# K and Q stored with the head's dimension first: PE's transposes of them against DMAs between halves of SBUF

## The chip, the cores and the metric

The kernel runs on one core of a Trainium2 chip. The metric is the device time of one execution in microseconds (us). All matrix work is done by TensorE (PE, with its weight loads shown as PEld); VectorE (DVE), ScalarE (ACT) and GpSimd (POOL) do the rest, and SyncE (SP) issues every DMA.

## The reference

Attention with pooled queries, then two feed-forward layers. B, H, S, D = 2, 8, 1152, 64.

```python
q_pool = q.reshape(B, H, S // 2, 2, D).mean(axis=3)
scores = scale * np.matmul(q_pool, k.transpose(0, 1, 3, 2))
attn = softmax(scores)                      # over S = 1152 keys
x = np.matmul(attn, v)                      # (B, H, 576, D) -> (1152 tokens, 512)
h = x @ w_in;  g = h * tanh(softplus(h));  x = g @ w_out      # 512 -> 2048 -> 512
h = x @ w_in2; g = elu(h);                 out = g @ w_out2
```

All tensors are float32 outside; the weights come as 64-bit floats and are converted on the chip.

## The kernel before

The attention goes through 8 pairs of heads (`n`). A pair has 9 query tiles of 128 rows: four of head 0 and four of head 1, alternating, and a last one made of the two heads' 64 remaining queries (`order`). The loop `while s < len(tiles)` takes one such tile as a step `s`, and each step works on several tiles at once: `qk` multiplies tile s (three blocks of 384 keys, in `A` banks of PSUM), DVE's `scores` scales it into `sp` and takes the maximum, ACT's `exp(s - 1)` and POOL's `norm(s - 1)` finish the tile before, and `trans(s - 3)` turns the tile three steps back on PE (in `B` banks), from which `probs` copies it to `pt`. `av` multiplies the turned probabilities with V; it runs in steps 1, 3, 5 and 8 of a pair, in portions of 8 or 10 products. Programs are in order on each engine; there is no planner here, and the order of the calls in the loop is the order on each engine.

The products of Q and K are made exact enough by splitting every number in two float32r halves, high and low. K is the moving operand: `KA` holds head 0's high half in partitions 0 to 63 and its low half in 64 to 127, `KB` head 1's, the other way round. Q is the stationary operand: `Q[h, 0]` is the high half of head h in both halves of the partitions, `Q[h, 1]` the low half.

K and Q come from memory with the tokens in the partitions. So for the next pair, in steps 3, 7 and 8 (`prep_k`) and 5 and 10 (`prep_q`), PE turns 9 blocks of K and 4.5 of Q into the single `D` bank; ACT rounds the high halves out of it (L246, L272), DVE subtracts for the low halves (L248, L274), and POOL copies each Q half to the other half of the partitions (L281). `pool_q` adds neighbouring queries first, on POOL (L229). In the steps with such work DVE, not ACT, copies the middle third of `probs` (`more`).

Eight chunks of weights are also converted during the attention (`Weights`: read in step 7 of a pair, `rebias` on ACT two steps later, `clamp` on POOL, `shift` and `words` on DVE, `high` on ACT, `rest` on POOL). `mlps` does the two layers in 48 units each; a unit is 12 products of `h_mm` (L172) and 9 or 12 of `out_mm` (L573), with the chunks converted ahead through a ring of NR = 4 raw buffers.

Of the kernel before, what the change touches and what calls it, by code (L numbers as in the profile page):

```python
# [22 lines left out]
def tile_pool_attention_mish_elu_mlp(  # L23
# [13 lines left out]

    nc = tc.nc
    B, H, S, D = q.shape
    NT, DM = out.shape  # L40
    DFF = moe_w_in.shape[1]
    P = 128
# [15 lines left out]
    NR = 4  # L58
# [83 lines left out]
    BANKS = {"A": 3, "B": 3, "C": 1, "D": 1}  # L142
    sums = cycle(("B", "B", "B", "C", "D"))
# [33 lines left out]
    def attention():  # L177
        with ExitStack() as st:
            ap = st.enter_context(tc.tile_pool(name="attn", bufs=2))
            pools["f"] = st.enter_context(tc.tile_pool(name="f1", bufs=2))  # L180
            raw_k, raw_q, ks, qs_t, vs = {}, {}, {}, {}, {}

            def load_k(n, pieces=1):
                b, h0 = n // NP, 2 * (n % NP)
                raw_k[n] = ap.tile([P, KT, 2, D], F32, tag="kr", name="kr", bufs=1)
                w = KT // pieces
                for c in range(pieces):
                    for h in range(2):
                        src = k[b, h0 + h].rearrange("(p t) d -> p t d", p=P)
                        t = slice(c * w, (c + 1) * w)  # L190
                        yield nc.sync.dma_start(out=raw_k[n][:, t, h, :], in_=src[:, t, :])

            def load_q(n, pieces=1):
                b, h0 = n // NP, 2 * (n % NP)
                qr = ap.tile([P, 2, 2 * NQ, D], F32, tag="qr", name="qr", bufs=1)
                qe = ap.tile([QR, 2, 2, D], F32, tag="qe", name="qe", bufs=1)
                raw_q[n] = [qr, qe]
                src = q[b, h0:h0 + 2, :2 * NQ * P].rearrange("h (p r) d -> p h r d", p=P)
                w = 2 * NQ // pieces
                for c in range(pieces):  # L200
                    r = slice(c * w, (c + 1) * w)
                    yield nc.sync.dma_start(out=qr[:, :, r, :], in_=src[:, :, r, :])
                yield nc.sync.dma_start(
                    out=qe, in_=q[b, h0:h0 + 2, 2 * NQ * P:].rearrange("h (p r) d -> p h r d", r=2)
                )
# [5 lines left out]

            def pool_q(n, eng, heads, t0=0, t1=NQ):

                if n not in qs_t:
                    qs_t[n] = Q = {}
                    raw_q[n] += [
                        ap.tile([P, NQ, 2, D], F32, tag="qs", name="qs", bufs=1),
                        ap.tile([QR, 2, D], F32, tag="qse", name="qse", bufs=1),
                    ]
                    for h in range(2):  # L220
                        for part in range(2):
                            Q[h, part] = ap.tile([P, NQ * P + P], F32R, tag=f"Q{h}{part}", name=f"Q{h}{part}")
                            z0 = NQ * P + (QR if h == 0 else 0)
                            nc.gpsimd.memset(Q[h, part][:, z0:z0 + QR].bitcast(F32), 0.0)
                qr, qe, qs, qse = raw_q[n]
                qv = qr.rearrange("p h (t r) d -> p h t r d", r=2)
                t = slice(t0, t1)
                for h in heads:
                    eng.tensor_tensor(qs[:, t, h, :], qv[:, h, t, 0, :], qv[:, h, t, 1, :], op=ALU.add)  # L229
                if t1 == NQ and 1 in heads:  # L230
                    eng.tensor_tensor(qse, qe[:, :, 0, :], qe[:, :, 1, :], op=ALU.add)


            left = {"act": [], "dve": [], "pool": []}

            def prep_k(n, g, bank="D"):
                kr = raw_k[n]
                if g == 0:
                    ks[n] = [ap.tile([P, S], F32R, tag=t, name=t) for t in ("KA", "KB")]
                KA, KBt = ks[n]  # L240
                pt = psum(bank)
                for i in range(3):
                    nc.tensor.transpose(pt[:, i * P:(i + 1) * P], kr[:, 3 * g + i], ident)  # L243
                c = slice(g * KB, (g + 1) * KB)
                for a, (r, o) in ((KA, (slice(0, D), slice(D, P))), (KBt, (slice(D, P), slice(0, D)))):
                    left["act"].append(lambda a=a, r=r: nc.scalar.copy(a[r, c], pt[r, :KB]))  # L246
                    left["dve"].append(
                        lambda a=a, r=r, o=o: nc.vector.tensor_tensor(a[o, c], pt[r, :KB], a[r, c], op=ALU.subtract)  # L248
                    )

            def prep_q(n, g, bank="D"):
                qs, qse = raw_q[n][2:]
                Q = qs_t[n]
                pt = psum(bank)
                t0, t1 = (0, NQ // 2) if g == 0 else (NQ // 2, NQ)
                w = 0
                for t in range(t0, t1):
                    nc.tensor.transpose(pt[:, w:w + P], qs[:, t], ident)  # L258
                    w += P
                if g == 1:  # L260
                    nc.tensor.transpose(pt[:, w:w + QR], qse, ident[:QR, :QR])  # L261
                    w += QR
                for h in range(2):
                    r, r2 = slice(h * D, (h + 1) * D), slice((1 - h) * D, (2 - h) * D)
                    pieces = [(slice(t0 * P, t1 * P), slice(0, (t1 - t0) * P))]
                    if g == 1:
                        if h == 0:
                            pieces = [(slice(t0 * P, t1 * P + QR), slice(0, w))]
                        else:
                            pieces.append((slice(t1 * P + QR, t1 * P + P), slice(w - QR, w)))  # L270
                    for o, i in pieces:
                        left["act"].append(lambda h=h, o=o, i=i, r=r: nc.scalar.copy(Q[h, 0][r, o], pt[r, i]))  # L272
                        left["dve"].append(
                            lambda h=h, o=o, i=i, r=r: nc.vector.tensor_tensor(  # L274
                                Q[h, 1][r, o], pt[r, i], Q[h, 0][r, o], op=ALU.subtract
                            )
                        )
                    o = slice(pieces[0][0].start, pieces[-1][0].stop)
                    for x in range(2):
                        left["pool"].append(  # L280
                            lambda h=h, x=x, o=o, r=r, r2=r2: nc.gpsimd.tensor_scalar(  # L281
                                Q[h, x][r2, o], Q[h, x][r, o].bitcast(F32), 1.0, 1.0, op0=ALU.mult, op1=ALU.mult
                            )
                        )

            def leave(*engines, most=99):
                for e in engines:
                    for f in left[e][:most]:
                        f()
                    del left[e][:most]  # L290
# [8 lines left out]
            def qk(s, j):  # L299
                n, i = tiles[s]  # L300
                KA, KBt = ks[n]
                Q = qs_t[n]
                sc[s, j] = pt = psum("A")
                c = slice(j * KB, (j + 1) * KB)
                if order[i] is None:
                    cols = slice(NQ * P, NQ * P + P)
                    terms = [(Q[0, 0], KA), (Q[0, 1], KA), (Q[1, 0], KBt), (Q[1, 1], KBt)]
                else:
                    h, t = order[i]
                    cols = slice(t * P, (t + 1) * P)  # L310
                    terms = [(Q[h, 0], (KA, KBt)[h]), (Q[h, 1], (KA, KBt)[h])]
                for x, (qq, kk) in enumerate(terms):
                    nc.tensor.matmul(pt[:, :KB], qq[:, cols], kk[:, c], start=(x == 0), stop=(x == len(terms) - 1))  # L313
# [72 lines left out]
            loads, preps, avs = {}, {}, {}  # L386
            for n in range(n_pairs):
# [6 lines left out]
                if n + 1 < n_pairs:  # L394
                    for r, f in (0, load_k), (-4, load_q):
                        loads.setdefault(s0 + r, []).append(lambda f=f, n=n: list(f(n + 1)))
                    loads.setdefault(s0 + 4 + LAG, []).append(lambda n=n: load_v(n + 1))
                    for r, f, g in zip(
                        (3, 5, 7, 8, 10),
                        (prep_k, prep_q, prep_k, prep_k, prep_q), (0, 0, 1, 2, 1),  # L400
                    ):
                        preps[s0 + r] = (f, n + 1, g)
            going = []
            pieces = [(x, y) for x in range(NW) for y in range(2)]


            kk, qq = load_k(0, 3), load_q(0, 2)
            for g in (qq, kk, kk, kk, kk, kk, kk, qq, qq):
                next(g)
            load_v(0)  # L410
# [297 lines left out]
```

## Time and profile before

| | us |
|---|---|
| median of 3 runs (lowest to highest) | 677.01 (677.01 to 677.14) |
| the profiled execution's own time | 677.06 |
| its span, from the first to the last instruction | 675.3 |
| PE busy | 659.9 (98%) |
| DVE, ACT, POOL busy | 502.6 (74%), 432.0 (64%), 218.7 (32%) |
| granted TensorE clock over the span | 1.00 |

The span is what the engines' records cover; the 1.76 us by which the execution is longer lie before and after them. A share of busy time is an average over the attention, which ends at 270 us, and the two layers. PE's matmuls are pipelined, so what an instruction costs is read from the chain of waits (the distance from one to the next), not from its own duration.

### The profile page before, as it was taken

The page shows a single profiled execution, that of the slowest core. Times are in us where ns is not written, and L with a number is a line of the kernel's source. Part 1 is how long each engine was busy: PE and PEld are TensorE (multiplying, and loading weights), DVE is VectorE, ACT ScalarE, POOL GpSimd, SP SyncE. Part 2 cuts the span into 40 slices and gives each one's busy share as a digit, 9 for nine tenths or more (in the row PEclk, how much of TensorE's full clock was granted, in tenths as well). Part 3 has the DMA queues.
Part 4 walks back from the last instruction along what each step waited for, and adds up shares of the span by engine and source line. Part 5 has one row for each costly group of instructions (what it writes and reads, how often), then busy time and mean ns, then how long its engine had stood idle before and what let it go on. Part 6 is the DMA issues. An engine that isn't in the chain of part 4 may idle for free.

```text
span 675.3 us, 11241 instructions
## 1 busy us (share of the span) xinstructions
PE 659.9 (98%) x3976; PEld 583.0 (86%) x3976; DVE 502.6 (74%) x1273; ACT 432.0 (64%) x895; POOL 218.7 (32%) x294
## 2 busy tenths in 40 slices
PE   6899999999999999999999999999999999999997
PEld 4777777777787776999999999999999999999995
DVE  5988888898989883846645765776987788996553
ACT  5888887888888886643443545445666566665442
POOL 2746566565747454211110431333310011110000
PEclk9999999999999999999999999999999999999999
DMA  6313140504130410413124222222211221200111
GB/s 175 102 37 104 34 123 16 137 15 125 36 102 1 160 33 33 124 64 125 64 62 125 63 94 82 75 94 63 93 64 64 93 94 64 94 33 1 47 48 47
DMA packets 47400, 50.79 MB, mean 75 GB/s; under 512 B 20336, under 2 KB 38256, under 8 KB 47344
## 3 DMA queue, kind: packets, MB, share of 16 engines
q1 hardware_dynamic: 47344, 50.08, 24.1%
q8 instruction: 31, 0.51, 0.3%
q14 instruction: 25, 0.20, 0.1%
HBM read 47.71 MB, written 2.36 MB: 74 GB/s over the span
## 4 chain that ended last, share of the span: by engine, by line
PE 96%; DVE 2%; issue 1%; POOL 0%; DMA 0%; ACT 0%; POOLq 0%
PE A L172 30%; PE B L573 18%; PE A L313 13%; PE C L367 11%; PE B L342 11%; PE D L573 6%; PE C L573 6%; PE D L243 1%; DVE sp L319 1%; PE D L258 1%; DMA qr<-in_q_dram 0%; DVE Q L274 0%; DVE part L598 0%; POOL Q L281 0%; PE D L261 0%
## 5 line engine op out<-in xcount | busy, mean ns | idle before, releaser
L172 PE MATMUL A<-XH,wl 128*128 128x384 f32 x384 | 128.9, 336 | 0.0
L172 PE MATMUL A<-XH,wh 128*128 128x384 f32 x384 | 128.8, 336 | 0.0
L172 PE MATMUL A<-XL,wh 128*128 128x384 f32 x384 | 128.6, 335 | 0.0
L319 DVE TENSOR_SCALAR_CACHE_REDUCE sp<-A 128x384 f32<-128x384 f32 x216 | 113.7, 554 | 17.1 <-PE A L313 13.7
L116 POOL TENSOR_SCALAR wf<-wf 128x512 f32<-128x512 f32 x64 | 42.7, 668 | 253.4 <-ACT wf L112 219.7
L336 POOL TENSOR_SCALAR sp<-sp,stat 128x1152 f32<-128x1152 f32 x72 | 91.8, 1275 | 100.0 <-DVE stat L335 87.8
L342 PE MATMUL B<-ident,sp 128*128 128x128 f32 x648 | 105.7, 273 | 4.3 <-POOL Q L281 3.6
L358 ACT COPY pt<-B 128x384 f32<-128x384 f32 x187 | 81.1, 485 | 23.4 <-PE B L342 22.3
L330 ACT ACTIVATE sp<-sp,stat 128x1152 f32<-128x1152 f32 x72 | 90.9, 1262 | 6.3 <-DVE stat L326 5.7
L342 PEld LDWEIGHTS B<-ident,sp 128*128 128x128 f32 x648 | 80.8, 140 | 14.5 <-POOL Q L281 5.9
L367 PE MATMUL C<-pt,vr 128*64 128x320 f32 (+1 forms) x576 | 76.7, 411 | 0.0
L527 ACT ACTIVATE gh<-A 128x384 fp32r<-128x384 f32 x48 | 23.7, 493 | 80.2 <-PE A L172 80.1
L172 PEld LDWEIGHTS A<-XH,wh 128*128 128x128 f32 x384 | 72.1, 188 | 2.5 <-issue 0.5
L313 PE MATMUL A<-KA,Q 128*128 128x384 f32 x240 | 73.5, 390 | 0.3 <-DVE KA L248 0.2
L172 PEld LDWEIGHTS A<-XL,wh 128*128 128x128 f32 x384 | 72.1, 188 | 1.9
L172 PEld LDWEIGHTS A<-XH,wl 128*128 128x128 f32 x384 | 72.0, 188 | 0.0
L313 PE MATMUL A<-KB,Q 128*128 128x384 f32 x240 | 70.5, 376 | 1.3 <-DVE sp L319 1.3
L367 PEld LDWEIGHTS C<-pt,vr 128*64 128x64 f32 x576 | 38.5, 136 | 27.7 <-issue 5.0
L530 DVE TENSOR_TENSOR gl<-g,gh 128x384 fp32r<-128x384 f32 x48 | 31.1, 649 | 34.7 <-ACT g L528 34.6
L553 ACT CAST gh<-g 128x384 fp32r<-128x384 f32 x48 | 24.7, 514 | 48.1 <-DVE g L547 47.8
L127 DVE SCALAR_TENSOR_TENSOR wf<-raw,wf 128x512 int32<-128x512 int32 x64 | 51.6, 806 | 2.2
L313 PEld LDWEIGHTS A<-KA,Q 128*128 128x128 f32 x240 | 37.6, 196 | 13.8 <-issue 9.5
(109 smaller groups left out, 1317.7 us busy)
## 6 DMA issues: line engine op xcount, KB each, us to landing
raw<-in_moe_w_in_dram SPq DMA_DIRECT2D x32, 512.0 KB, 3.8
raw<-in_moe_w_out_dram SPq DMA_DIRECT2D x32, 512.0 KB, 3.3
vr<-in_v_dram SPq DMA_DIRECT2D x8, 576.0 KB, 4.1
kr<-in_k_dram SPq DMA_DIRECT2D x14, 288.0 KB, 4.0
qr<-in_q_dram SPq DMA_DIRECT2D x7, 512.0 KB, 3.9
out_dram<-part SPq DMA_DIRECT2D x8, 256.0 KB, 2.2
kr<-in_k_dram SPq DMA_DIRECT2D x6, 96.0 KB, 2.8
qr<-in_q_dram SPq DMA_DIRECT2D x2, 256.0 KB, 3.1
```

Source lines behind the costliest of these rows:

```text
L116: nc.gpsimd.tensor_scalar(self.f, self.f, HUGE, -HUGE, op0=ALU.min, op1=ALU.max)
L127: nc.vector.scalar_tensor_tensor(f, self.low, 29, f, op0=ALU.logical_shift_right, op1=ALU.bitwise_or)
L172: nc.tensor.matmul(pt[:, :TB], w[:, kk * P:(kk + 1) * P], x[:, kk, tk], start=(i == 0), stop=(i == len(terms) - 1))
L313: nc.tensor.matmul(pt[:, :KB], qq[:, cols], kk[:, c], start=(x == 0), stop=(x == len(terms) - 1))
L319: nc.vector.tensor_scalar(sp[s][:, j * KB:(j + 1) * KB], sc.pop((s, j))[:, :KB], SCALE, None, op0=ALU.mult, op1=ALU.max, accum_out=stat[s] ...
L330: nc.scalar.activation(sp[s], sp[s], AF.Exp, bias=m[:, 3:4], scale=1.0, accum_out=m[:, 4:5])
L336: nc.gpsimd.tensor_scalar(sp[s], sp[s], m[:, 6:7], 1.0, op0=ALU.mult, op1=ALU.mult)
L342: nc.tensor.transpose(pt[:, x * P:(x + 1) * P], sp[s][:, c:c + P], ident)
L358: copy(dst, src)
L367: nc.tensor.matmul(acc[n, g][h * D:(h + 1) * D, :w], vs[n][:, h, kt, :], pts[n, g][:, kt, h, :], start=(kt == 0), stop=(kt == KT - 1),)
L530: nc.vector.tensor_tensor(gl, g, gh, op=ALU.subtract)
L573: nc.tensor.matmul(pt, l, r, start=(first and i == 0), stop=(final and i == 2))
```

## The change

The host hands K and Q over with the head's dimension first, and Q's even and odd queries apart; the odd heads' Q is rotated by 64 so that its leftover queries come first. PE turns neither. For a next pair, K (both heads, one per half of the partitions) and Q come with one DMA each. POOL adds the query halves, ACT rounds all 128 partitions at once, POOL subtracts, and then SP issues six DMAs from SBUF to SBUF, each of 64 partitions by 4,608 bytes (295 KB): three bring Q's halves of each head into both halves of the partitions, three exchange head 0's low half of K and head 1's high half through the raw buffer. `PREP` gives the step of each. The first pair is loaded instead with every head twice, once into each half, in fourteen DMAs, and needs no moves; the second head's raw tiles borrow `sp` buffers. Besides: the `D` bank goes to `B` (4 banks), the raw ring shrinks from 4 to 3, `probs`' middle third goes to DVE except for three of nine tiles, and the output's rows lie one after another.

```diff
-    NR = 4
+    NR = 3
...
-    BANKS = {"A": 3, "B": 3, "C": 1, "D": 1}
-    sums = cycle(("B", "B", "B", "C", "D"))
+    BANKS = {"A": 3, "B": 4, "C": 1}
+    sums = cycle(("B", "B", "B", "B", "C"))
...
-            pools["f"] = st.enter_context(tc.tile_pool(name="f1", bufs=2))
+            pools["f"] = st.enter_context(tc.tile_pool(name="f1", bufs=1))
...
+            def load_k0(h, blocks=(0, 3)):
+                if h not in raw_k:
+                    raw_k[h] = ap.tile([P, S], F32, tag="sp" if h else "kr", name="kr", bufs=LAG + 1 if h else 1)
+                c = slice(blocks[0] * KB, blocks[1] * KB)
+                for r in range(2):
+                    nc.sync.dma_start(out=raw_k[h][r * D:(r + 1) * D, c], in_=k[0, h, :, c])
...
+            def prep_q0(h, pool, low, cols):
+                x, c, o = raw_q[h], slice(*cols), slice(cols[0] + h * QR, cols[1] + h * QR)
+                hi, lo = (qs_t[0][h][:, part, o] for part in range(2))
+                pool.tensor_tensor(x[:, 0, c], x[:, 0, c], x[:, 1, c], op=ALU.add)
+                nc.scalar.copy(hi, x[:, 0, c])
+                low.tensor_tensor(lo, x[:, 0, c], hi, op=ALU.subtract)
+
+            def prep_k0(h, j):
+                K, c, r = ks[0][h], slice(j * KB, (j + 1) * KB), slice(D, P)
+                nc.scalar.copy(K[:, c], raw_k[h][:, c])
+                nc.vector.tensor_tensor(K[r, c], raw_k[h][r, c], K[r, c], op=ALU.subtract)
...
+            def pool_q(n):
+
+                tiles_of(n)
+                x = raw_q[n]
+                nc.gpsimd.tensor_tensor(x[:, 0], x[:, 0], x[:, 1], op=ALU.add)
+
+            def high_q(n):
+                nc.scalar.copy(qs_t[n][0][:, 0, :SQ], raw_q[n][:, 0])
+
+            def low_q(n, eng):
+                x = qs_t[n][0]
+                eng.tensor_tensor(x[:, 1, :SQ], raw_q[n][:, 0], x[:, 0, :SQ], op=ALU.subtract)
+
+            def move_q(n, i):
+                x, y = qs_t[n]
+                src = x[(0 if i == 2 else D):(D if i == 2 else P), :, :SQ]
+                dst = (y[D:, :, QR:], y[:D, :, QR:], x[D:, :, :SQ])[i]
+                nc.sync.dma_start(out=dst.bitcast(F32), in_=src.bitcast(F32))
+
+            def high_k(n, i):
+                c = slice(i * S // 2, (i + 1) * S // 2)
+                nc.scalar.copy(ks[n][0][:, c], raw_k[n][:, c])
+
+            def low_k(n, i, eng):
+                c = slice(i * S // 2, (i + 1) * S // 2)
+                eng.tensor_tensor(ks[n][1][:, c], raw_k[n][:, c], ks[n][0][:, c], op=ALU.subtract)
+
+            def move_k(n, i):
+
+                (x, y), t = ks[n], raw_k[n][:D]
+                src, dst = ((x[D:], t), (y[:D], x[D:]), (t, y[:D]))[i]
+                nc.sync.dma_start(out=dst.bitcast(F32), in_=src.bitcast(F32))
...
+            PREP = [
+                (0, "pool", pool_q, ()), (1, "act", high_q, ()), (2, "pool", low_q, (nc.gpsimd,)),
+                (3, "sp", move_q, (0,)), (3, "sp", move_q, (1,)), (4, "sp", move_q, (2,)),
+                (2, "act", high_k, (0,)), (3, "act", high_k, (1,)),
+                (3, "pool", low_k, (0, nc.gpsimd)), (4, "pool", low_k, (1, nc.gpsimd)),
+                (5, "sp", move_k, (0,)), (6, "sp", move_k, (1,)), (7, "sp", move_k, (2,)),
+            ]
...
-                    for r, f in (0, load_k), (-4, load_q):
-                        loads.setdefault(s0 + r, []).append(lambda f=f, n=n: list(f(n + 1)))
-                    loads.setdefault(s0 + 4 + LAG, []).append(lambda n=n: load_v(n + 1))
...
+                    for r, f in (-3, load_q), (-1, load_k), (4 + LAG, load_v):
+                        loads.setdefault(s0 + r, []).append(lambda f=f, n=n: f(n + 1))
+                    m = n + 1
+                    for r, e, f, args in PREP:
+                        preps.setdefault((s0 + r, e), []).append(lambda f=f, args=args, m=m: f(m, *args))
...
+            load_q0(0, cut[0])
+            load_k0(0, (0, 1))
+            load_k0(0, (1, 3))
+            load_q0(1, cut[1])
+            load_k0(1)
+            load_q0(0, (cut[0][1], SQ))
+            load_q0(1, (cut[1][1], SQ))
             load_v(0)
...
+            for h in range(2):
+                prep_q0(h, nc.vector if h == 0 else nc.gpsimd, nc.vector, cut[h])
+                for j in range(3):
+                    prep_k0(h, j)
+            for h in range(2):
+                prep_q0(h, nc.gpsimd, nc.gpsimd, (cut[h][1], SQ))
...
-                    if s in preps and 1 == j:
-                        f, n, g = preps.pop(s)
-                        f(n, g)
...
-                    for j in range(3):
-                        if j != 1 or not more:
-                            probs(o, j, nc.scalar.copy)
+                    probs(o, 0, nc.scalar.copy)
+                    probs(o, 2, nc.scalar.copy)
+                for f in by["act"]:
+                    f()
...
-                if old and (1 in [j for _, j in tp]):
-                    probs(o, 1, nc.vector.tensor_copy)
+                if old:
+                    probs(o, 1, nc.scalar.copy if o % NI in (0, 1, 3) else nc.vector.tensor_copy)
+                for e in "dve", "pool", "sp":
+                    for f in by[e]:
+                        f()
```

## Rows read from the trace of the kernel before

**Rows 1.** The page: the chain that ended last, by line.

```profile
PE A L172 30%; PE B L573 18%; PE A L313 13%; PE C L367 11%; PE B L342 11%; PE D L573 6%; PE C L573 6%; PE D L243 1%; DVE sp L319 1%; PE D L258 1%; DMA qr<-in_q_dram 0%; DVE Q L274 0%; DVE part L598 0%; POOL Q L281 0%; PE D L261 0%
```

**Rows 2.** Windows by pair: start:end, length, engines' busy us, clock, DMA share.

```profile
0.00:35.27 35.27, 26.53 (x141) 21.01 (x143) 26.48 (x97) 24.77 (x49) 18.04 (x39) 1.00 0.47 133
...
195.24:227.23 31.99, 31.66 (x230) 24.83 (x231) 28.11 (x103) 27.33 (x58) 19.39 (x26) 1.00 0.32 92
227.23:257.35 30.12, 30.12 (x218) 23.68 (x220) 24.40 (x95) 24.83 (x53) 15.07 (x15) 1.00 0.10 32
```

**Rows 3.** Chain of waits in pair 3: start us, length us, engine, tile, line.

```profile
104.82 0.22 PE D L258 x2
105.04 0.20 PE D L261
105.24 0.48 PE B L342 x3
...
111.56 0.33 PE D L243 x3
...
128.01 0.33 issue
128.34 0.52 PE B L342 x3
```

**Rows 4.** Chain of waits in pair 7, which prepares no next pair's K.

```profile
229.54 0.55 PE A L313 x2
...
231.78 0.35 PE A L313 x2
...
243.39 0.55 PE A L313 x2
```

**Rows 5.** Groups of instructions by line: busy us, mean ns of one, idle before.

```profile
L342 PE MATMUL B<-ident,sp 128*128 128x128 f32 x648 | 105.7, 273 | 4.3 <-POOL Q L281 3.6 <-issue 0.7
...
L135 ACT CAST wh<-wf 128x512 fp32r<-128x512 f32 x64 | 39.7, 620 | 5.2 <-DVE wf L127 5.2
...
L281 POOL TENSOR_SCALAR Q<-Q 64x256 fp32r<-64x256 f32 (+2 forms) x64 | 27.3, 441 | 6.5 <-ACT Q L272 3.9
...
L358 DVE COPY pt<-B 128x384 f32<-128x384 f32 x29 | 16.2, 557 | 0.5
...
L229 POOL TENSOR_TENSOR qs<-qr 128x256 f32<-128x256 f32 (+1 forms) x16 | 13.7, 861 | 1.4 <-DMA qr<-in_q_dram 0.8
...
L138 POOL TENSOR_TENSOR wl<-wf,wh 128x512 fp32r<-128x512 f32 x8 | 10.3, 1281 | 4.6 <-ACT wh L135 4.6
```

**Rows 6.** DMA queue and issues: KB each, median us from issue to landing.

```profile
q1 hardware_dynamic: 47344, 50.08, 24.1%
...
vr<-in_v_dram SPq DMA_DIRECT2D x8, 576.0 KB, 4.1
...
out_dram<-part SPq DMA_DIRECT2D x8, 256.0 KB, 2.2
...
out_dram<-part SPq DMA_DIRECT2D x2, 128.0 KB, 2.3
```

**Rows 7.** Chain of waits of the first 36 us: by line, two steps.

```profile
by line: PE A L313 20.5%; PE B L342 11.3%; DVE sp L319 10.4%; DMA qr<-in_q_dram 7.9%; issue 6.8%; DVE Q L274 6.1%; POOL Q L281 4.9%; DVE KB L248 4.3%; POOL sp L336 3.4%; DVE KA L248 3.2%; PE C L367 2.2%; ACT Q L272 2.1%; PE B L258 1.9%; PE 
...
10.69 0.58 DVE sp L319 x2
...
17.99 0.33 PE B L342 x3
```

**Rows 8.** Timeline of the start: first uses of the two halves of Q.

```profile
3.60 0.49 DVE L229 TENSOR_TENSOR qs<-qr 128x128 f32<-128x128 f32 x2 [3.60 <-DMA qr<-in_q_dram]
...
7.90 0.87 POOL L229 TENSOR_TENSOR qs<-qr 128x128 f32<-128x128 f32 x2 [0.79 <-DMA qr<-in_q_dram]
```

**Rows 9.** Timeline of SP in the second layer: a chunk is read.

```profile
585.78 0.37 SPq L100 DMA_DIRECT2D raw<-in_moe_w_in_dram  x1
```

**Rows 10.** Timeline of ACT there: the chunk before that one is converted.

```profile
591.03 0.68 ACT L112 ACTIVATE wf<-raw 128x512 f32<-128x512 f32 x1 [0.45 <-DVE wl L138]
```

More of the change, by code (lines that the diff above doesn't have):

```diff
@@ L193, in load_q, with tiles_of @@
-            def load_q(n, pieces=1):
-                b, h0 = n // NP, 2 * (n % NP)
[L195 to L205, printed above, removed]
+            def tiles_of(n):
+                ks[n] = [ap.tile([P, S], F32R, tag=t, name=t) for t in ("KA", "KB")]
+                qs_t[n] = [ap.tile([P, 2, SQ + QR], F32R, tag=f"Q{h}", name=f"Q{h}") for h in range(2)]
+                for h in range(2):
+                    z0 = 0 if h else SQ
+                    nc.gpsimd.memset(qs_t[n][h][:, :, z0:z0 + QR].bitcast(F32), 0.0)
@@ new lines, in load_k0, with load_q0 @@
+            def load_k0(h, blocks=(0, 3)):
[4 more added lines that the diff above has]
+                    nc.sync.dma_start(out=raw_k[h][r * D:(r + 1) * D, c], in_=k[0, h, :, c])
+            def load_q0(h, cols):
+                if h not in raw_q:
+                    x = ap.tile([P, S], F32, tag="sp" if h else "qr", name="qr", bufs=LAG + 1 if h else 1)
+                    raw_q[h] = x.rearrange("p (a s) -> p a s", a=2)
+                c = slice(*cols)
+                for r in range(2):
+                    nc.sync.dma_start(out=raw_q[h][r * D:(r + 1) * D, :, c], in_=q[0, h, :, :, c])
@@ new lines, in load_k, with load_q @@
+            def load_k(n):
+                b, h0 = n // NP, 2 * (n % NP)
+                raw_k[n] = ap.tile([P, S], F32, tag="kr", name="kr", bufs=1)
+                nc.sync.dma_start(out=raw_k[n], in_=k[b, h0:h0 + 2].rearrange("h d s -> (h d) s"))
+            def load_q(n):
+                b, h0 = n // NP, 2 * (n % NP)
+                x = ap.tile([P, S], F32, tag="qr", name="qr", bufs=1)
+                raw_q[n] = x.rearrange("p (a s) -> p a s", a=2)
+                nc.sync.dma_start(out=raw_q[n], in_=q[b, h0:h0 + 2].rearrange("h d a s -> (h d) a s"))
@@ L210, in load_v @@
                 nc.sync.dma_start(out=vs[n], in_=v[b, h0:h0 + 2].rearrange("h (p t) d -> p h t d", p=P))
[L212 to L231, printed above, removed]
@@ L234, in attention @@
[L234 to L249, printed above, removed]
@@ L251, in prep_q @@
[L251 to L290, printed above, removed]
             order = [(h, t) for t in range(NQ) for h in range(2)] + [None]
@@ L440, in attention @@
                     av(*a)
-                more = left["dve"] and not any(w.age == 4 for w in going)
+                by = {e: preps.pop((s, e), []) for e in ("act", "dve", "pool", "sp")}
                 if mid:
                     exp(s - 1)
-                leave("act")
                 if old:
-                    for j in range(3):
-                        if j != 1 or not more:
-                            probs(o, j, nc.scalar.copy)
+                    probs(o, 0, nc.scalar.copy)
+                    probs(o, 2, nc.scalar.copy)
+                for f in by["act"]:
+                    f()
                 if new:
@@ L451, in attention @@
                     scores(s, 1)
-                if new:
                     scores(s, 2)
@@ L463, in attention @@
                         tokens(n, g)
-                if 2 <= s % NI < 2+2 and s // NI + 1 < n_pairs:
-                    pool_q(s // NI + 1, nc.gpsimd, (s % NI - 2,))
                 for w in list(going):
```

57 lines of the change are left out of this document (18 added, 39 removed).

## The prediction

> **What bounds the kernel now.** I first read the page's chain that ended last [rows 1]: nearly all of it is PE, and the lines of the attention (L313, L342, L367) are a third. So work taken from PE is worth its time, if nothing else becomes late. To see whether that holds where the change acts, I cut the attention where the av of step 8 begins, once per pair, and read the busy time of each piece [rows 2]. A pair takes 31.99 us and PE is busy for 31.66 of them; DVE is busy for 28.11, ACT for 27.33, POOL for 19.39. Pair 7, the last, has no next pair's K to prepare and only the second half of its own Q: it takes 30.12 us and PE is never idle. That pair is a run of the new PE program which the trace already holds. The chain inside a pair [rows 3, 4] then shows what the 1.87 us between the two consist of.
>
> This document reckons with the profiled execution's own 677.06 us (span 675.3 and 1.76 around it); the median of the runs is 677.01, so the two agree within 0.05.
>
> **What leaves PE.** Three K blocks are one piece of 0.33 us in the chain, three times a pair: 0.98. The second half of Q takes 0.22 and 0.20, and the three probability turns behind it take 0.48 instead of 0.33: 0.57. The first half of Q is two turns like the 0.22. In step 8 PE then waits 0.33 for probabilities, and the turns behind the wait take 0.52 instead of 0.33: 0.52 in all [rows 3]. Of all waits of these turns most is put down to POOL's Q copies, 3.6 us, since POOL's normalisation is queued behind them; the copies go too (L281, 0.44 us each, 8 a pair [rows 5]). Sum: 0.98 + 0.57 + 0.22 + 0.52 = 2.29 us a pair. The windows say the same from the other side: pair 7 without its 0.57 us is 30.12 - 0.57 = 29.55 us, and 31.99 - 29.55 = 2.44. I take 2.44, which holds the small waits as well. Pairs 1 to 6 gain it in full: 6 x 2.44 = 14.6 us. Pair 7 gains 0.57. Sum 15.2 us. The turns of pair 0 are in the start's term below.
>
> **What comes to the other engines.** ACT gets three roundings of 128 x 576 per pair in place of the K and Q roundings; a 128 x 512 one takes 0.62 [rows 5], so 0.7 each, 2.1 in all. Even on top of pair 7's 24.83 us [rows 2] that is 26.9 of 29.55. DVE loses every subtraction for K and Q and gets the middle `probs` copies of six tiles instead of one in pair 7: 24.40 + 5 x 0.56 [rows 2, 5] = 27.2 of 29.55, its Q subtractions not yet taken off. POOL gets one sum and three subtractions of 576 columns. A 128 x 512 two-input instruction takes 1.28 and 256 columns take about 0.86 [rows 5]: 1.4 to 1.9, say 1.5 each, 6 a pair. Against that go its Q copies (8 x 0.44) and sums (2 x 0.9): POOL stays near 20. In the fullest steps (3 and 4) POOL does a normalisation of 1.2, a subtraction of 1.5 and once a weight's 1.28, up to 4.0 us, but a tile's normalisation is called two steps before its turn. So each of them is cheap because PE's work covers it; without the cover ACT would cost most, since it stands ahead of exp.
>
> **The moves.** Each subtraction of low halves ends on POOL, then SP moves 295 KB three times in a row for K, each waiting for the one before. In pair 7 step 0 opens at 229.54, step 1 at 231.78 and step 4 at 243.39 [rows 4]. So step 4 opens 13.85 after step 0; POOL then has its normalisation (1.2) and the last K subtraction (1.5), with some waiting: done at about 17.2. Head 1's K is needed when the next pair's step 1 opens, 29.55 + 2.24 = 31.8. That leaves 14.6 us for three moves, 4.9 each. No row shows a move in SBUF. The nearest are a 256 KB store in 2.2 us and a 576 KB load in 4.1 [rows 6]; bounds 2.2 and 4.1, and I take 3.5, nearer to the load since load_q, load_v and a weight read share the queue. Third move done at 17.2 + 10.5 = 27.7, 4.1 us early: cost 0, and 0 at both bounds. Q's moves start after step 2 and have longer. What waits behind a move on SP is load_v, the weight read and load_k; load_k comes last, at 27.7, lands 4.1 later and is used in step 2 of the next pair. Nothing on PE's path.
>
> The Trainium skill speaks against this part: SBUF — State Buffer, section Door 1, says that a DMA on 64 partitions reaches half the ports, 196 GB/s measured against 328 with 128, and that every DMA pays about 2 us besides. An estimate by it makes a move 2 us + 295 KB / 196 GB/s = 3.5 us, still within 4.9. The trace's 64-partition store of 128 KB takes 2.3 us against 2.2 for twice the bytes on 128 partitions [rows 6], which fits it.
>
> **The start.** Before, the first scores are at 10.69 and the first turned probabilities at 17.99; from there to the 35.27 us at which pair 0's window ends [rows 2, 7] DVE's and POOL's Q work still holds the chain. Their shares of these 36 us are 6.1% and 4.9%, 3.9 us together [rows 7]. What replaces them is loads. DVE, in order, subtracts head 1's K before it takes the first scores, and by then 1.77 MB must have come (every head twice: 0.26 and 0.33 of Q, 0.59 and 0.59 of K), where 1.1 MB had come by 7.90 before. Two rates bound it: from the landing of 0.26 MB at 3.60 to 1.11 MB at 7.90 [rows 8], 0.2 MB per us; and the queue's 50.08 MB over 675.3 us at a share of 24.1% [rows 6], 0.31. So head 1's K lands at 8.5 to 11.2, and with 2.2 us of ACT and DVE the first scores are at 10.7 to 13.4: 0 to 2.7 later. There is a second wait. load_q of pair 1 needs the buffer that POOL empties with the last of head 0's Q (that part lands at 9.5 to 12.8 by the same rates, and sum, rounding and subtraction take 1.0, 0.5 and 1.0); it lands 4.1 later, pool_q takes 1.5, and only then POOL normalises tile 0 (1.2), since pool_q stands ahead of it. ACT's exp(1) is queued behind the rounding that waits for the same sum. First turns at 18.8 to 22.1 against 17.99: 0.8 to 4.1 late. Taken off are the 3.9 us, less what of them lies before 17.99 (about one). So the start ends between 2.1 early and 1.2 late. I take 0.
>
> **The layers.** The five sum banks stay five. With NR = 3 a read is issued when the words of three reads back are done, which is when the next read was issued before. The tightest I find of 56: issue at 585.78 [rows 9], conversion of the chunk at 591.03 [rows 10], 5.2 us for a landing that takes under 4.1. Cost 0. Without that cover ACT's queue would wait, one late chunk at a time. The end of the program, with its last stores, is unchanged.
>
> **The rivals.**
> One, the loads of the start: as in the forecast, but the doubled 64-partition loads go below the slower of the two rates, and pair 1's K moves, made late by that, hold its step 1 as well. First scores 3 to 4 late, one wait of 2 to 3 more: 4 to 7 us, time 666 to 669. For it: both queues of waits above are in series. Against: only pair 0 has them.
>
> By the same section of the Trainium skill's SBUF — State Buffer, head 1's K would land at an estimated 3.6 + 1.51 MB / 196 GB/s = 11.3 us, about my slower bound of 11.2.
>
> Two, another engine takes the path: ACT (26.9) or DVE (27.2) cannot follow at 29.55 because their work is uneven; a pair stops at about 30.8. Gain 7 x 1.2 = 8, time 669. For it: DVE and ACT are busy for 85 to 88% of a pair now [rows 2]. Against: pair 7 ran at 82% without a wait.
>
> Three, slower: the moves come late. At 4.9 us each they meet step 1; beyond that each pair waits 3 us per us of move, and the gain of 2.44 is gone at 5.7. At 6.2 us a pair loses 3 x 1.3 - 2.44 = 1.5, seven pairs 10: 687. For it: three in series, and no row of one. Against: a load of twice the size takes 4.1.
>
> Four, the change does not do what it says: the turns were covered, PE waits elsewhere, 677. Against: PE idles 0.33 of 31.99 us.
>
> **How the numbers follow.** Forecast 677.06 - 15.2 + 0 = 661.9, say 662, chance 0.74; its own range, with the start's bounds and half a microsecond of small waits, 659 to 664. Rival one 0.10, two 0.07, three 0.05, four 0.04. The range 658.5 to 667 holds the forecast and the lower half of rival one, 0.8. Faster by over 0.2% (1.4 us, about what a measurement of this kernel tells from no change) are the forecast and rivals one and two, 0.91; within it rival four and a move of 5.7 us, 0.04; slower 0.05.
>
> **What would show it.** The same windows should give pairs of 29.5 to 29.8 us with PE idle under 0.3. No L243, L258 turns; PE instructions 112 fewer. Pair 0's first av of step 8 at 33 to 37 us. The third K move should land before step 1 of the next pair; a wait of PE's weight load or of qk for a DMA of K or Q in each pair means rival three, waits for ACT or DVE rival two, a pair 0 over 38 us rival one. The layers should take the same 405 us. The prediction is wrong if a move takes over 5 us, or if the first norm comes after 24 us.

## The result, and the profile after

The changed kernel takes 669.04 us (median of 4 runs, 668.31 to 669.83), the kernel before 677.01 beside it: ratio 0.9882, 95% interval 0.9865 to 0.9899. It is faster, by 8.0 us where 15.2 were forecast, and 2 us above the range's upper end. The profiled execution is 669.11 (span 667.3).

The same cut as in [rows 2], of the kernel after, at each pair's first av of step 8 (columns as there):

```profile
0.00:36.84 36.84, 22.25 (x114) 19.20 (x114) 22.78 (x86) 22.92 (x44) 19.58 (x26) 0.95 0.55 149
36.84:68.95 32.11, 30.56 (x216) 23.47 (x217) 24.28 (x94) 23.65 (x47) 19.61 (x17) 1.00 0.55 154
...
159.50:189.79 30.29, 30.00 (x216) 23.50 (x217) 24.18 (x94) 23.67 (x47) 19.57 (x17) 1.00 0.50 136
...
220.05:249.77 29.72, 29.72 (x215) 23.41 (x217) 24.12 (x94) 22.07 (x44) 13.21 (x11) 1.00 0.29 97
```

Pair 7 has what was forecast for every pair, all but 0.17. Pairs 2 to 6 take 151.10 us together, 3.35 above five times 29.55; pair 1 is 2.56 above, pair 0 1.57 above its 35.27. From there to the end it is 0.37 shorter than before. 1.57 + 2.56 + 3.35 + 0.17 - 0.37 = 7.3: this is the gain that is missing (the profiled executions, 677.06 and 669.11, differ by 7.95 of 15.2). The busy times of DVE, ACT and POOL are all below their bounds in the prediction, so no engine is full; what is late must be late by order, or by a wait within the pair.

The page's chain by line, which was PE almost alone before [rows 1]:

```profile
PE 80%; DVE 8%; DMA 6%; ACT 2%; issue 1%; SPq 1%; POOL 1%; POOLq 0%; ACTq 0%
```

The chain of waits in pair 5 says where DMA, ACT and DVE enter it (start, length, what):

```profile
158.99 6.62 DMA raw<-in_moe_w_in_dram
...
165.63 0.02 ACT wf L114
...
168.20 0.68 ACT Q L242
168.88 0.28 ACT XH L360
...
171.94 1.25 DVE wf L123
...
175.69 1.60 DVE wf L129
177.29 0.48 DVE sp L298 x2
```

Read it from below: PE waits for scores (sp) that stand behind DVE's word operations on a weight (wf), DVE is late from XL, which waits for ACT's XH (the low and high halves of the attention's result), ACT is late because its conversion of the weight (L114) waited for the read. And the read? SP's timeline:

```profile
151.76 0.48 SPq L266 DMA_DIRECT2D kr<-KA  x1
154.79 0.48 SPq L266 DMA_DIRECT2D KA<-KB  x1
155.32 0.58 SPq L233 DMA_DIRECT2D qr<-in_q_dram  x1
157.85 0.46 SPq L266 DMA_DIRECT2D KB<-kr  x1
158.35 0.59 SPq L271 DMA_DIRECT2D vr<-in_v_dram  x1
158.99 0.92 SPq L102 DMA_DIRECT2D raw<-in_moe_w_in_dram  x1
163.06 0.34 SPq L227 DMA_DIRECT2D kr<-in_k_dram  x1
```

The weight read (raw) is called in step 7 as before, but gets through the queue only behind the third K move. Its conversion on ACT, due two steps after the call, was 13 us behind the issue before, as SP's and ACT's timelines show:

```profile
91.16 0.46 SPq L100 DMA_DIRECT2D raw<-in_moe_w_in_dram  x1
...
104.20 0.67 ACT L112 ACTIVATE wf<-raw 128x512 f32<-128x512 f32 x1
```

In after it is 6.6 behind, the whole of the transfer. The moves themselves are on time, though with little to spare; the groups of DMA issues (KB each, median us to landing):

```profile
kr<-KA SPq DMA_DIRECT2D x7, 288.0 KB, 3.0
KA<-KB SPq DMA_DIRECT2D x7, 288.0 KB, 3.0
KB<-kr SPq DMA_DIRECT2D x7, 288.0 KB, 3.5
```

The load of K at 163.06 waits for the third move, which so took 5.2 us here (157.85 to 163.04), and PE needed its result at 163.84.

The waits by engine and releaser from 36 to 260 us (us in total, times, longest) name a second cause on ACT, its rounding of Q behind POOL's sum:

```profile
ACT wf L114 <- DMA raw<-in_moe_w_in_dram: 4.8, 3, 2.8
...
PE A L292 <- DVE sp L298: 2.5, 7, 0.9
...
ACT Q L242 <- POOL qr L239: 1.7, 2, 0.9
```

The start: first the chain of the first 37 us, then windows of it (the last three columns: granted clock, DMA share, GB/s):

```profile
15.14 3.48 DMA qr<-in_q_dram
...
18.79 1.41 POOL qr L239
...
20.29 1.24 POOL sp L315
...
21.57 0.55 PE B L321 x3
```

```profile
5.00:10.00 5.00, 2.41 (x6) 1.64 (x6) 2.01 (x4) 2.06 (x5) 0.90 (x1) 1.00 0.97 252
...
20.00:25.00 5.00, 3.43 (x15) 3.23 (x16) 2.26 (x11) 4.42 (x8) 3.72 (x4) 0.70 0.00 0
```

The first turned probabilities come at 21.57 against 17.99 [rows 7], behind pair 1's Q sum, as the prediction's second wait had it. New is the granted clock of 0.70: PE, which had waited 4.60 us up to 14.85 and 2.24 up to 21.57, then ran its pieces at half speed (three turns take 0.64 there, 0.33 later).

### The profile page after: what moved, and what is told of

It reads as the page before. It is cut to its first block, busy times and chain, and to the rows that moved or that the text cites. A ratio compares the mean times of both kernels' runs of the same rounds, so it can differ in the third digit from the quotient of the medians.

```text
span 667.3 us, 10816 instructions
## 1 busy us (share of the span) xinstructions
PE 645.3 (97%) x3864; PEld 572.6 (86%) x3864; DVE 476.8 (71%) x1211; ACT 404.4 (61%) x819; POOL 219.0 (33%) x223
## 4 chain that ended last, share of the span: by engine, by line
PE 80%; DVE 8%; DMA 6%; ACT 2%; issue 1%; SPq 1%; POOL 1%; POOLq 0%; ACTq 0%
PE A L174 30%; PE B L553 24%; PE A L292 8%; PE B L321 6%; PE C L346 6%; PE C L553 6%; DVE sp L298 3%; DMA raw<-in_moe_w_in_dram 3%; DVE wf L129 1%; DMA qr<-in_q_dram 1%; DVE wf L123 1%; ACT sp L309 1%; DMA Q<-Q 1%; DMA kr<-KA 1%; DVE wf L128 1%
## 5 line engine op out<-in xcount | busy, mean ns | idle before, releaser
L298 DVE TENSOR_SCALAR_CACHE_REDUCE sp<-A 128x384 f32<-128x384 f32 x216 | 112.1, 552 | 19.8 <-PE A L292 16.9
L321 PEld LDWEIGHTS B<-ident,sp 128*128 128x128 f32 x648 | 83.5, 141 | 11.9 <-POOL sp L315 3.4
L337 ACT COPY pt<-B 128x384 f32<-128x384 f32 x168 | 75.2, 485 | 29.7 <-PE B L321 28.7
L507 ACT ACTIVATE gh<-A 128x384 fp32r<-128x384 f32 x48 | 23.7, 493 | 80.2 <-PE A L174 80.2
L346 PEld LDWEIGHTS C<-pt,vr 128*64 128x64 f32 x576 | 38.5, 136 | 27.7 <-issue 4.2
L510 DVE TENSOR_TENSOR gl<-g,gh 128x384 fp32r<-128x384 f32 x48 | 31.9, 667 | 34.7 <-ACT g L508 34.6
```

Of the source, the lines that this page charges most:

```text
L298: nc.vector.tensor_scalar(sp[s][:, j * KB:(j + 1) * KB], sc.pop((s, j))[:, :KB], SCALE, None, op0=ALU.mult, op1=ALU.max, accum_out=stat[s] ...
L321: nc.tensor.transpose(pt[:, x * P:(x + 1) * P], sp[s][:, c:c + P], ident)
L337: copy(dst, src)
L346: nc.tensor.matmul(acc[n, g][h * D:(h + 1) * D, :w], vs[n][:, h, kt, :], pts[n, g][:, kt, h, :], start=(kt == 0), stop=(kt == KT - 1),)
L510: nc.vector.tensor_tensor(gl, g, gh, op=ALU.subtract)
```

## The experiments

The theories to be told apart: (A) the weight read behind the moves, (B) ACT's rounding of Q ahead of XH, (C) DVE's word operations, (D) the start's loads, (E) the start's wait for pair 1's Q. Each median is that of the kernel's own runs, each ratio is against runs of the kernel before on the same chip. The lengths come from each profile's timeline: where the first av of step 8 begins; the windows above begin up to 0.07 us later.

| kernel | us | ratio | pair 0 | pair 1 | pairs 2-6, mean | pair 7 |
|---|---|---|---|---|---|---|
| before | 677.01 | | 35.2 | 31.96 | 32.00 | 30.12 |
| after | 669.04 | 0.9882 | 36.8 | 32.05 | 30.22 | 29.72 |
| e1 read early | 666.78 | 0.9846 | 37.2 | 29.99 | 30.04 | 29.72 |
| e2 round late | 667.73 | 0.9860 | 37.4 | 32.01 | 30.15 | 29.72 |
| e3 no words | 666.27 | 0.9841 | 37.8 | 31.36 | 29.56 | 29.52 |
| e4 start wide | 666.53 | 0.9843 | 34.7 | 31.96 | 30.04 | 29.73 |
| e5 two queues | 667.76 | 0.9866 | 37.5 | 31.64 | 30.09 | 29.75 |
| e7 sum later | 671.43 | 0.9918 | 37.2 | 34.37 | 30.19 | 29.75 |
| e8 convert late | 687.21 | 1.0150 | 37.3 | 33.44 | 32.64 | 31.60 |
| e9 all | 686.72 | 1.0147 | 35.7 | 33.70 | 32.61 | 31.60 |
| e10 words in step 8 | 669.99 | 0.9891 | 37.0 | 29.63 | 30.04 | 29.76 |
| e11 Q load free | 667.21 | 0.9852 | 35.4 | 32.19 | 30.08 | 29.72 |
| e12 early, free | 662.45 | 0.9785 | 34.6 | 29.81 | 29.73 | 29.73 |
| e13 one queue | 663.34 | 0.9794 | 35.4 | 29.82 | 29.74 | 29.75 |

Pair 0 of the six profiles with an unchanged start lies between 36.8 and 37.8, so differences under 1 us tell little there in a single profile.

**e1, the read ahead of the moves (A).**

```
-                if pieces and s % NI == 7:
+                if pieces and s % NI == 2:
                     going.append(Weights(*pieces.pop(0)))
+                    going[-1].age = -5
```

`age` counts the steps behind the read, and ACT's conversion comes at 2: with -5 it stays in the step where it was.

> The attention's weight read is issued in step 2 of a pair instead of step 7, ahead of all moves; its conversion steps stay. Theory (late read): ACT's wait for the weight words, 4.8 us over three pairs in the changed kernel, goes; pair 1, 32.1 us long there, comes down to 30.2 to 30.7, the pairs 2 to 6 (30.2) lose 0.1 or 0.2 each; time 666.3 to 667.3 against 669.0. Rival (pair 1 is long because the start was late, or because DVE is full in the steps 1 to 4): pair 1 stays above 31.5 and the time within 0.5 of 669.0. Rival (transfers disturb each other): the read meets the moves of Q instead, and the time rises by 1 or more.

Pair 1 fell by 2.06, and ACT's waits for the weight are gone from its profile; 2.3 us by the medians. A holds: pair 1 was not long because of the late start, which this run has too. Not all of the 2.06 is the read's: 0.4 of after's pair 1 is PE's wait for the third K move (KB, 0.17 us of idle time at 41.63), and it is absent here, where pair 0 ends 0.4 later. Pairs 2 to 5 keep 29.98.

**e2, the rounding of Q behind XH (B).**

```
-                (0, "pool", pool_q, ()), (1, "act", high_q, ()), ...
+                (0, "pool", pool_q, ()), (1, "late", high_q, ()), ...
...
                         tokens(n, g)
+                for f in by["late"]:
+                    f()
```

> ACT's rounding of the next pair's Q, which waits for POOL's sum, is issued behind the rounding of the attention's result (XH) in the same step instead of ahead of it. Theory (ACT's queue): XH, then XL and DVE's next scores, come 0.5 to 1 us earlier in pairs 2 to 6; these go from 30.2 to 29.9 or 30.0 us, in all 1.0 to 1.5 us less: 667.5 to 668.0. Rival (DVE's own work in the steps 1 to 4 sets it, whenever XH comes): pairs within 0.1 of 30.2, time 668.5 to 669.5. Pair 1 stays at 32 by both.

Pairs 3 to 6 took 29.72 to 29.76, as long as pair 7, which rounds no Q; pair 1 and, in this run, pair 2 (31.79) still paid for the late read. B holds by the pairs: 29.98 - 29.73 = 0.25 each. The median is 1.3 below after's, but there the two intervals overlap.

**e3, no shift and no word operations (C).**

```
-            if wide:
+            if wide and self.x >= NW:
```

in `shift` and `words`.

> DVE's shift and two word operations on the weight chunks that are read in the attention (3.6 us a pair) are left out; nothing takes their place, so the result is not the reference's. Theory (DVE's stretch): without them DVE has caught up by step 3 in every pair; PE's waits for DVE's scores go, pairs 2 to 6 fall to 29.7 to 29.8, pair 1 by less than 1 as its wait is ACT's; time 665.5 to 667. Rival (what is late on ACT reaches PE whatever DVE does): pairs 2 to 6 stay at 30.1 or more, time above 668.

PE's waits for DVE are gone after pair 1, and pairs 2 to 5 and 7 take 29.52: without DVE's conversion neither B nor A reaches PE there, so both come through DVE, which with the conversion has no slack in the steps 1 to 4. In pair 1 ACT's late conversion reaches PE without it (31.36). The 0.2 below pair 7's 29.72 is what DVE's conversion costs even where nothing else is late.

**e4, wide loads for pair 0 (D).** `in_=k[0, 0:2, :, c]` to all 128 partitions in place of two loads of `k[0, h, :, c]` to 64 each; the same for Q.

> Each pair of 64-partition loads of the first pair becomes one 128-partition load of as many bytes, 7 for 14; the lower half of the partitions gets head 0's and the upper half head 1's values in both heads' buffers, so pair 0's result is not the reference's. Theory (issue): SP needs about 0.6 us for each issue, and seven fewer of them bring head 1's K in from 11.4 to 7.5 to 8.5 us, the first scores from 14.1 to 10.5 to 11.5, pair 1's Q sum and the first turned probabilities by 2 to 3; pair 0 ends at 33.5 to 35.0 instead of 36.8; time 666 to 667.5. Rival (bytes): the same bytes take as long, first scores after 13, pair 0 36.3 or more, time 668.5 to 669.5.

Pair 0's end is within the theory's bounds, but not by its reason. The window of this kernel that stands against 5 to 10 us of after:

```profile
5.00:10.00 5.00, 3.02 (x6) 1.50 (x6) 3.26 (x6) 2.40 (x6) 0.90 (x1) 1.00 1.02 376
```

In both the 16 DMA engines are busy all the time (0.97, 1.02); with 128 partitions they move 376 GB/s, with 64 only 252. In these 5 us the engines, not SP's 0.6 us for each issue, were the limit; in the first 5 us of after their share is 0.35, so there they were not. The first scores came at 12.05, later than the theory's 10.5 to 11.5.

**e5, three of the loads on ACT's queue (D).**

```
+                    eng = nc.scalar if r > h else nc.sync
-                    nc.sync.dma_start(out=raw_k[h][r * D:(r + 1) * D, c], ...)
+                    eng.dma_start(out=raw_k[h][r * D:(r + 1) * D, c], ...)
```

and so for Q's first part.

> Of the fourteen 64-partition loads of pair 0 the three that fill the upper half for head 0's first Q and K go to ACT's DMA queue; the other eleven stay on SP. Bytes and shapes are those of the changed kernel. Theory (issue on one queue): three issues less ahead of head 1's K bring it in from 11.4 to about 9.6 us, the first scores to 12.3, pair 0's end from 36.8 to 35.0 to 35.8; time 667.0 to 668.0. Rival (half-width transfers): the loads are limited by their 64 partitions and not by SP; head 1's K within 0.5 of 11.4, time 668.5 to 669.5.

The first scores came at 13.51 instead of 14.13 (the theory had 12.3), DMA moved 270 GB/s from 5 to 10 us, and pair 0 was no shorter. The time is in the theory's range, but its interval overlaps that of after, and the profile does not show where it would come from: inconclusive alone (see e13).

**e7, pair 1's Q preparation one step later (E).**

```
+                        if m == 1 and f in (pool_q, high_q, low_q, move_q):
+                            r += 1
```

> Pair 1's whole Q preparation (POOL's sum, ACT's rounding, POOL's subtraction, three moves) is called one step later, so that POOL's normalisation of tile 0 and ACT's exp of tile 1 are ahead of the sum and the rounding that wait for pair 1's load; other pairs as they were. Theory (order on POOL): the first turned probabilities come at 18 to 19 us instead of 21.6, PE's low clock between 20 and 25 us (0.70 there) goes or shortens, pair 0 ends at 34.5 to 35.5; time 667 to 668. Rival (the first scores at 14.1 set it): the first turns come at most 1 us earlier and later waits for the sum take it back; time 668.5 to 669.5. Against the theory also: Q's moves one step later push K's moves, pair 1 waits 1 or more for K and the time is above 669.5.

The theory fell. POOL normalised tile 0 at 18.49 instead of 20.29, but the sum then stood in the way of the next tiles, and pair 0 ended at 37.25. Q's later moves pushed K's: the first was issued at 32.61 instead of 31.18, the third at 40.59 instead of 38.23. PE then waited for K in pair 1 (waits of PE, 37 to 72 us):

```profile
PE A L292 <- DMA KA<-KB: 1.1, 1, 1.1
```

Another 1.2 us of PE's waiting, up to 44.18, is put down to a DVE copy, but the third move landed only at 44.05. That is rival three's mechanism, reached with 2.4 us of delay; and the weight read behind the moves was later by as much (41.73 for 39.37).

**e8, the conversion three steps later (A, C).** `going[-1].age = -3` after the read.

> The weight read stays where it is, behind the moves, but each step of its conversion comes three steps later (ACT in step 3 of the next pair instead of 0, DVE in steps 5 and 6 instead of 2 and 3). Theory (late read, and DVE full in steps 1 to 4): pair 1 comes to 30.0 as in the run with the early read, and the pairs 2 to 6 lose 0.2 more as DVE's conversion leaves the steps in which tokens and scores are late: 29.75 to 29.9; time 665.0 to 666.3. Rival (the read itself disturbs the moves): pair 1 above 31. Rival (DVE is as full in the steps 5 and 6): pairs 2 to 6 at 30.0, time 666.5 to 667.3.

Both the theory and its rivals fell: every pair from 1 to 7 lost 1.2 to 3.2 us against after. The chain in its pair 3:

```profile
128.02 0.60 DVE wf L128
128.64 1.60 DVE wf L129
130.24 0.49 DVE sp L298 x2
130.77 1.07 PE A L292 x4
131.84 0.64 PE B L321 x3
132.48 1.28 PE A L292 x4
```

```profile
128.00:131.00 3.00, 1.21 (x9) 0.93 (x8) 2.97 (x6) 2.56 (x5) 1.49 (x1) 1.00 0.80 200
131.00:135.00 4.00, 4.00 (x17) 3.81 (x17) 2.55 (x12) 1.71 (x3) 2.47 (x2) 0.57 0.95 277
```

DVE's 2.2 us, called in step 6, stand ahead of step 7's scores. PE is busy for 1.21 of 3 us, and then, in four of the seven pairs (1, 3, 5 and 6, the long ones), the granted clock falls, to 0.57 here, and three turns take 0.64.

**e9, e2 + e5 + e7 + e8.**

> The late rounding of Q, the three loads on ACT's queue, the later sum for pair 1 and the late conversion together. If the causes are separate and add up: pair 0 ends at 33.5 to 35, pairs 1 to 7 at 29.55 to 29.75 each; time 661.5 to 664. If they share one cause, or the end of the attention now waits for the last weight conversion, 665 or more.

The sum missed by over 20 us: it has e8's pairs, and PE's waits for K from e7, so it does not tell whether the other causes add up.

**e10, the conversion five steps later.** `going[-1].age = -5`.

> As the run with the late conversion, but five steps later instead of three: ACT's conversion in step 5, DVE's shift in step 7 and its two word operations in step 8, the rounding and POOL's subtraction in step 0. Theory (step length): the late conversion cost 18 us because DVE's 2.2 us of word operations fell into step 6, which has no av and is only 2.2 us of PE long, where step 3 has 16 av and is over 4 long; step 8 has 20 av and no tokens, so there they cost nothing: pairs 1 to 6 at 29.7 to 30.0, no clock below 1.00 after the start, time 664.5 to 667. Rival (any conversion that runs beside the moves and the next pair's first roundings is late): pairs stay above 31, time above 678.

Pairs 1 and 2 took 29.6, pairs 3 to 6 30.16, with no clock below 1.00 after the start: moving the same work from step 6 to step 8 (20 av, as many as step 3 has) took e8's loss away, and the rival fell. The 0.5 us of pairs 3 to 6 are waits of PE's weight load, in the waits of PEld from 126.4 to 156.4 us:

```profile
PEld A L292 <- DVE sp L298: 0.4, 2, 0.2
```

The first, up to 130.93, is for scores behind DVE's words (128.09 to 130.40); the second, up to 137.32, is for scores behind XL, whose XH stands behind ACT's rounding of Q as in B. In pair 2 DVE reached its words 0.6 us earlier in the step; why is told below, with the shift. The time is no better than after's, for another reason: the last weight is now converted after the attention, and the first layer waits for it. The chain there:

```profile
269.71 0.69 DVE wf L129
270.41 0.89 DVE gl L511
...
271.34 2.21 PE B L554 x11
```

From the last pair's first av to the end it took 421.5 us, after 417.6.

**e11, pair 1's Q load without a wait (E).**

```
-  x = ap.tile([P, S], F32, tag="sp" if h else "qr", ...)
+  x = ap.tile([P, S], F32, tag="sp" if h else "vr", ...)
...
-            load_v(0)
             ...
+            load_v(0)
```

in `load_q0`, and `load_v(0)` behind pair 1's loads.

> Head 0's raw Q of pair 0 goes into a buffer that the second V tile uses later, so pair 1's load of Q no longer waits for POOL to empty it, and pair 0's V is loaded last. Theory (second wait of the start): pair 1's Q is in by 15 to 16.5 instead of 18.7, POOL's sum no longer holds back its normalisation of tile 0; the first turned probabilities come at 18.5 to 19.5 instead of 21.6, and PE's low clock (0.70 from 20 to 25 us) is shorter; pair 0 ends at 34.5 to 35.7; time 667.0 to 668.2. Rival (bytes): the same bytes come in whatever their order, the sum waits as long, or V is late; pair 0 at 36.5 or more, time 668.5 to 669.5.

Pair 0 shortened by 1.5, to 35.38. The chain of its start:

```profile
17.26 0.58 DVE sp L298 x2
...
18.95 1.24 POOL sp L315
...
20.23 0.58 PE B L321 x3
20.81 0.36 PE A L292 x2
```

The turns come at 20.23, not at 18.5 to 19.5: the sum is out of the chain, and DVE's scores of the next tile, ahead of the normalisation's small operations, hold it now. PE is back at 0.36 for two score matmuls at once, where after stayed at 0.60 to 0.66 until 25. E holds, with a smaller size.

**e12, e1 + e2 + e5 + e11.**

> The early weight read, the late rounding of Q, three loads on ACT's queue and pair 1's Q load without a wait, together; nothing is left out. If the causes are separate and add up: pair 0 ends at 33.5 to 35.5, pairs 1 to 7 at 29.72 to 29.8 each, time 663.0 to 665.0. If they share a cause: 665.5 or more.

Its windows by pair:

```profile
34.55:64.36 29.81, 29.81 (x214) 23.35 (x213) 24.11 (x94) 23.49 (x47) 19.55 (x17) 1.00 0.59 164
...
183.28:213.01 29.73, 29.73 (x215) 23.41 (x214) 24.13 (x94) 23.49 (x47) 19.58 (x17) 1.00 0.46 119
```

PE has no gap left from pair 1 on. The four gains over after, taken from the medians of their own runs, are 2.3 + 1.3 + 1.3 + 1.8 = 6.7; together they gave 6.6. This kernel beats both, by 2.15% the kernel before (interval 2.01 to 2.29). What it shares with after (the raw ring of 3, the single `wf` buffer, four `B` banks, DVE's copies of `probs`) can so cost no more than the 0.18 by which a pair is above 29.55. Its time is the one predicted for the change, but in part by luck: 0.18 in seven pairs and 0.09 more in pair 1 are made good by a pair 0 that is 0.65 shorter than before's and an end 0.37 shorter.

**e13, e12 without the second queue.**

> The version with the early weight read, the late rounding of Q and pair 1's Q load without a wait, but with all loads of pair 0 on SP's queue again. If the second queue is worth what its own median says (1.3 us): time 663.5 to 664.2, the first scores at 14.1 instead of 13.5, pair 0 ending near 35.4. If its own run's gain was only the spread between executions: 662.2 to 663.0, pair 0 within 0.4 of 34.55.

663.34, and pair 0 ends at 35.36 for 34.55: 0.9 by the medians, between the two expectations. The first scores (14.22 for 13.46) say it is the queue, but both differences are within the spread of pair 0 and the intervals overlap; a gain of about 1 is likely, not shown.

## Why the prediction missed, by its own steps

**What leaves PE: right.** 112 PE instructions fewer. Where nothing stands in the way a pair takes 29.73 (e12), 29.52 without DVE's conversion (e3), forecast 29.55. Pair by pair that is 2.26 to 2.47 less than 31.99, forecast 2.44.

**The moves: cost 0 nearly right, the margin and the sentence on what waits behind them wrong.** K's moves took 3.0 to 3.5 us by their medians, forecast 3.5. The estimate by the Trainium skill (SBUF — State Buffer, Door 1 and The DMA setup-cost knee) was also 3.5. But the third took 5.2 in two pairs, over the 5 us that the prediction named as a sign of being wrong, and the first started some 20 us after step 0 opened, not 17.2 (161.80 and 181.99 in pair 5), since POOL's last subtraction ends only then. So the third move was 0.1 to 2.8 us early, not 4.1; PE waited for one once (pair 1, 0.2 us idle, 0.4 in its chain).

The first step that failed is "load_k comes last, at 27.7, lands 4.1 later and is used in step 2 of the next pair. Nothing on PE's path." load_k was followed to its use, and the weight read, named in the same sentence, was not. Its conversion is due in the next pair's step 0, earlier than load_k's use in step 2, and it stands on ACT ahead of exp and XH. Cost: up to 2.1 us in pair 1, 2.3 in all (e1).

**What comes to the other engines: loads right, cost 0 wrong.** ACT 23.7, DVE 24.3, POOL 19.6 in a pair, below the bounds 26.9, 27.2 and about 20. The second step that failed is "each of them is cheap because PE's work covers it": it was argued from sums over a pair. Within it, ACT's new rounding waits for POOL in front of XH (e2: 0.25 a pair, in pairs 3 to 6), and DVE's conversion lies where DVE has no slack (e3: 0.2 a pair). DVE's conversion also became longer. Two of its groups by line, in pairs 2 to 7 of after, then its shift in pairs 2 to 6 of before:

```profile
L129 DVE SCALAR_TENSOR_TENSOR wf<-raw,wf 128x512 int32<-128x512 int32 x6 | 9.6, 1602 | 0.2
...
L123 DVE TENSOR_SCALAR wf<-wf 128x512 int32<-128x512 int32 x6 | 8.0, 1329 | 0.0
...
L121 DVE TENSOR_SCALAR wf<-wf 128x512 int32<-128x512 int32 x5 | 2.0, 408 | 0.0
```

The shift takes 1.33 us where it took 0.41 before; the second word operation took 1.60 before too, and takes 0.71 in the layers, where POOL does little. In pair 5 the shift begins at 171.86, 0.18 us behind the start of POOL's normalisation (171.68 to 172.91), and ends 0.28 behind its end; in before it began 0.28 ahead of one (111.17 and 111.45). e10, where POOL subtracts nothing beside it, has both orders in one trace:

```profile
64.72 0.43 DVE L123 TENSOR_SCALAR wf<-wf 128x512 int32<-128x512 int32 x1
64.78 1.47 POOL L315 TENSOR_SCALAR sp<-sp,stat 128x1152 f32<-128x1152 f32 x1
...
94.17 1.23 POOL L315 TENSOR_SCALAR sp<-sp,stat 128x1152 f32<-128x1152 f32 x1 [0.18 <-DVE stat L314]
...
94.35 1.33 DVE L123 TENSOR_SCALAR wf<-wf 128x512 int32<-128x512 int32 x1
```

So it is in all thirteen traces that have the shift in the attention, up to 262 us: 22 shifts that begin while POOL is idle take 0.41 to 0.43, and 85 that begin within a POOL instruction end 0.28 or 0.29 us behind that one's end, and so take 0.46 to 1.35. The Trainium skill (SBUF — State Buffer, SBUF: two separate sides) says that DVE, in a mode with two ports or with two inputs in SBUF, and POOL share one pair of ports and that the one that starts first holds it for its whole instruction, and the traces agree. In e10 this fits the difference between pair 2 and pairs 3 to 6 as well: the one short shift of its pairs is the one ahead of pair 2's words.

What these engines cost is rival two by its place, though not by its reason (load) nor its size (pairs at 30.8).

**The start: a size too small.** The term "I take 0" measured +1.57, above its bound of +1.2. Head 1's K, forecast to land at 8.5 to 11.2, was there at 11.4, about where the estimate by the Trainium skill (SBUF — State Buffer, Door 1) had it (11.3). ACT and DVE then took 2.7 us, forecast 2.2: the first scores at 14.13 lie above 10.7 to 13.4. The loads moved 100 GB/s in the first 5 us and 252 in the next, which is between the two rates taken (0.2 and 0.31 MB per us) but from a later start; the 196 GB/s of the Trainium skill (SBUF — State Buffer, Door 1) are below what was measured. This is the first half of rival one; its second half, late K moves, hardly came, since PE waited 0.2 us for K. The second wait is as foreseen (21.57, in 18.8 to 22.1; e11: 1.5 us). Not in the sum was the half clock after PE's waits; e11 and e12, which shorten them, don't have it beyond the first turns.

**The layers: right.** 405.1 us against 405.3.

The time of 669 equals that which rivals one and two named, but neither alone made it: late read 2.3, rounding 1.3, start 1.6 or more and DVE's conversion about 0.2 a pair share it. These are from separate runs and need not add up to 7.3.

## What to carry to other kernels

When a chain of dependent DMAs is put on an in-order queue, follow every transfer behind it to the instruction that needs it and to that instruction's own queue; the harmful one was the smallest and the only one with no relation to the change. Busy time below the span of a stage proves no cover: check it step by step, since the same 2.2 us of DVE cost 0.2 us in a step with av work, and 1.8 or more, with a clock drop behind it, in one without. After removing work from the bounding engine, look for what is now just in time; here four changes of order, queue and buffer (one of them, the queue, not shown to help by itself), none of them a saving of work, raised the gain from 8.0 to 14.6 us.

## What was not expected of the hardware

A DVE shift of 0.41 us lasted until 0.28 or 0.29 us behind the end of the POOL instruction within which it began, in 85 of 85 cases; begun 0.06 us ahead of it, it took 0.43. Loads to 64 partitions kept all 16 DMA engines busy (0.97) at 252 GB/s, where the same bytes to 128 partitions went at 376 (1.02). PE waited 1.8 us once in each pair of e8, and in four of the seven (1, 3, 5 and 6) some 4 us at a granted clock of 0.57 (0.65 in pair 6) followed; the waits of 0.3 us in after's pairs 2 to 6 were followed by none. In e5 the clock column shows 1.00 from 21 to 27 us, while three turns take 0.64 us there, and 0.33 later: a stretch at half speed is read from the durations too, not from the column alone.
